# Linear attention with a decayed state: from tiles of 128 tokens to blocks of 64 on 64x64 tiles of TensorE

## The chip, the cores and the metric

The kernel runs on one core of one Trainium2 chip. The metric is the device time of one launch in microseconds (us). Before the change it was 674.69 and 676.3 us in two runs, median 675.5. The profile is one execution, recorded by the hardware's profiler, with a span of 672.5 us. TensorE's clock was granted in full throughout it (mean 0.999).

## The reference

Two operations follow each other. The first is attention with a decay per head: no softmax, but a 64x64 state per head which is faded and added to from block to block. The second is a mixer: a product of low rank along the tokens, and then two dense layers with a ReLU between them. B is 4, H is 8, S is 768 tokens, D is 64. Cut to what matters:

```python
def _attn_ref(q, k, v, lam):              # q, k, v: (4, 8, 768, 64), float32
    block = 64
    ...
    Dmask = np.where(rel >= 0, lam[:, None, None] ** rel[None, :, :], 0.0)
    lam_pow = lam[:, None, None] ** (pos[None, :, None] + 1)
    lam_block = lam ** block
    for b in range(nb):
        qb, kb, vb = (q[:, :, sl], k[:, :, sl], v[:, :, sl])
        intra = np.einsum('bhic,bhjc->bhij', qb, kb) * Dmask[None]
        intra = np.einsum('bhij,bhjd->bhid', intra, vb)
        inter = np.einsum('bhid,bhde->bhie', qb * lam_pow[None], kv_state)
        out[:, :, sl] = intra + inter
        rev_pow = lam[:, None, None] ** (block - 1 - pos[None, :, None])
        kb_dec = kb * rev_pow[None]
        kv_state = lam_block * kv_state + np.einsum('bhsd,bhse->bhde', kb_dec, vb)

def _moe_ref(x, U, V, w_ch1, w_ch2):      # x: (4, 768, 512), U: (768, 32), V: (32, 768)
    h = x.transpose(0, 2, 1) @ U @ V
    u = x + h.transpose(0, 2, 1)
    ch = np.maximum(u @ w_ch1, 0.0) @ w_ch2      # 512 -> 2048 -> 512
    return u + ch
```

The block length is free: the same output comes out of any split of the tokens, if the decay inside a block goes into the mask and the decay across blocks into the scaling of q and k and into the state.

## The kernel before

The attention is computed in 24 steps, one for each tile of 128 tokens (6 tiles in each of 4 batches, `NT = 6`, `NS = 24`). A tile holds all 8 heads, as 4 pairs (`HP = 4`). All on-chip sums of this part lie in one pool, in eight banks: one each for the tags `pq`, `pk`, `pt` and `pu`, two for the scores `pss`, two for the output `px`.

```python
def turn_half(s, a0, name):               # transposes of q or k, then a copy by ScalarE
    ts, tag = (qts, ("pq", "pt")) if name == "q" else (kts, ("pk", "pu"))
    ...
    nc.tensor.transpose(out=pt[:, a - a0, :], in_=raw[s, name][:, 2 * a : 2 * a + 2, :], identity=ident)
    nc.scalar.copy(ts[s][:, a0 : a0 + n, :], pt)

def scale_k(s):                           # GpSimd: k times its reversed decay; none for a batch's last tile
    ...
def scale(s):                             # GpSimd: q times its decay; none for a batch's first tile
    ...
def fade(s):                              # ScalarE: the state times lam**128, 4 operations
    if 0 < s % NT < NT - 1:
        ...
def scores(s):
    st[s]["pss"] = pss = two_banks("pss", "pss").rearrange("p x (a i) -> p x a i", a=HP)
    for a in range(HP):
        for x in range(2):
            for rows in half if s >= 2 * NT else [slice(0, P)]:
                nc.tensor.matmul(out=pss[rows, x, a, :], lhsT=kt[half[x], a, rows],
                                 rhs=qt[half[x], a, :], start=True, stop=True)
def masked(s):                            # VectorE, one operation for each of two banks
    for x in range(2):
        nc.vector.tensor_tensor(out=sm[:, x], in0=pss[:, x], in1=mask[:, x], op=ALU.mult)
def state(s):                             # none for a batch's last tile
    if c < NT - 1:
        pkv = one_bank([P, HP, D], "pkv", "pk")
        for a in range(HP):
            for x in range(2):
                nc.tensor.matmul(out=pkv[half[x], a, :], lhsT=ks[:, a, x, :], rhs=vr[:, 2 * a + x, :],
                                 start=True, stop=True)
        ...
            nc.vector.tensor_tensor(out=kv[s + 1], in0=pkv, in1=st[s]["faded"], op=ALU.add)
def inter(s):                             # state times q; none for a batch's first tile
    for a in range(HP):
        for x in range(2):
            for t in range(2):
                nc.tensor.matmul(out=px[half[t], x, a, :], lhsT=st[s]["qs"][half[x], a, half[t]],
                                 rhs=kv[s][half[x], a, :], start=(a == 0), stop=False)
def intra(s):                             # masked scores times v, on top of inter
    for a in range(HP):
        for x in range(2):
            for t in range(2):
                nc.tensor.matmul(out=px[half[t], x, a, :], lhsT=sm[:, x, a, half[t]],
                                 rhs=vr[:, 2 * a + x, :], start=(first and a == 0), stop=(a == HP - 1))
    nc.scalar.copy(xs[s].rearrange("p (a x e) -> p x a e", a=HP, x=2), px)
```

Seven steps behind the attention, each tile of x gets its low-rank part (`mix`: one matmul into the bank `pu` and an addition by VectorE) and is turned and split for the dense layers (`turn`: four transposes into the bank `pt`, then VectorE, ScalarE and GpSimd). At a batch's first tile, `low` forms the low-rank rows of the batch before in the bank `pq`; `low_rows` and three `next_of_low` split them into a high and a low part. The weights' conversion (`aside`) is spread over the steps. The order of emission is fixed, and is the order in which each engine works:

```python
    step = [("prep", s + 1), ("scale", s + 1)] * more
    step += [("mix", done)] * (0 <= done < NS - NT - 1)              # done = s - NT - 1
    step += [("low", b - 1), ("low_rows", b - 1)]                     # c == 0 and b > 0 alone
    step += [("intra", s), ("next_of_low", b - 1), ("late", s), ("state", s), ("next_of_low", b - 1)]
    step += [("turned", done - 1), ("late", s), ("next_of_low", b - 1), ("scores", s + 1)]
    step += [("aside", s)] * (s >= 2 * NT)
    step += [("inter", s + 1), ("masked", s + 1), ("fade", s + 1)]
    step += [("aside", s)] * (s < 2 * NT) + [("turn", done)]
```

(The conditions of most pieces are left out here.) After the 24 steps come the two dense layers: 48 units of the hidden layer with 24 matmuls each, and 384 rounds of three matmuls for the output layer, each matmul with 512 columns. The change doesn't touch them.

Of the kernel before, what the change touches and what calls it, by code (L numbers as in the profile page):

```python
# [8 lines left out]
FP32 = mybir.dt.float32  # L9
# [5 lines left out]
P = 128  # L15
# [3 lines left out]
def kernel(  # L19
# [227 lines left out]

    def one_bank(shape, name, tag):
        return psf.tile(shape, FP32, tag=tag, name=name)
# [14 lines left out]
    def load(name, s, engine):  # L264
        b, c = divmod(s, NT)
        t = raw_pool.tile(
            [P, H, D], FP32, tag=f"{name}raw", bufs=4 if name == "k" else 3, name=f"{name}raw"
# [19 lines left out]
    small = consts.tile([P, 16], FP32, name="small")  # L287
# [8 lines left out]
    lamc = powq[:, :, P - 1 : P]  # L296

    def constants():
        for a in range(HP):
            for x in range(2):  # L300
                h = 2 * a + x
                nc.vector.tensor_tensor_scan(
                    mask[:, x, a, :], lamb[:, h : h + 1].broadcast_to([P, P]), ident, 0.0,
                    ALU.mult, ALU.add,
                )

    def powers():
# [5 lines left out]
        for a in range(HP):  # L313
            nc.vector.tensor_tensor_scan(
                powq[:, a, :], lamh[:, a : a + 1].broadcast_to([P, P]),
                zeros.broadcast_to([P, P]), 1.0, ALU.mult, ALU.add,
            )

# [10 lines left out]
    kv = {}  # L329
# [10 lines left out]
    def turn_half(s, a0, name):  # L340

        ts, tag = (qts, ("pq", "pt")) if name == "q" else (kts, ("pk", "pu"))
        if a0 == 0:
            ts[s] = att.tile([P, HP, P], FP32, tag=name + "t", bufs=2, name=name + "t")
        n = HP // parts(s)
        pt = one_bank([P, n, P], "p" + name, tag[a0 > 0])
# [5 lines left out]

    def prep(s):
        for a0 in range(0, HP, HP // parts(s)):
            for name in "qk":
                turn_half(s, a0, name)
        st[s].update(qt=qts.pop(s), kt=kts.pop(s))
        for name in "qk":
            load_next(name)

    def scale_k(s):
        st[s] = {}
        if s % NT < NT - 1:
            st[s]["ks"] = ks = att.tile([P, HP, 2, D], FP32, tag="ks", bufs=2, name="ks")
# [7 lines left out]
    def scale(s):  # L372

        if s % NT > 0:
            st[s]["qs"] = qs = att.tile([P, HP, P], FP32, tag="qs", bufs=2, name="qs")
            nc.gpsimd.tensor_tensor(out=qs, in0=st[s]["qt"], in1=powq, op=ALU.mult)  # L376
        if s + 1 < NS:
            scale_k(s + 1)

    def fade(s):  # L380

        if 0 < s % NT < NT - 1:
            st[s]["faded"] = faded = att.tile([P, HP, D], FP32, tag="faded", name="faded")
            for a in range(HP):
                nc.scalar.mul(faded[:, a, :], kv[s][:, a, :], lamc[:, a, :])

    def scores(s):
        qt, kt = st[s]["qt"], st[s]["kt"]
        st[s]["pss"] = pss = two_banks("pss", "pss").rearrange("p x (a i) -> p x a i", a=HP)
        for a in range(HP):  # L390
            for x in range(2):
                for rows in half if s >= 2 * NT else [slice(0, P)]:
                    nc.tensor.matmul(  # L393
                        out=pss[rows, x, a, :], lhsT=kt[half[x], a, rows],
                        rhs=qt[half[x], a, :], start=True, stop=True,
                    )

    def masked(s):
        pss = st[s].pop("pss")
        st[s]["sm"] = sm = att.tile([P, 2, HP, P], FP32, tag="sm", bufs=1, name="sm")  # L400
        for x in range(2):
            nc.vector.tensor_tensor(out=sm[:, x], in0=pss[:, x], in1=mask[:, x], op=ALU.mult)  # L402

    def state(s):
        c = s % NT
        if c < NT - 1:
            ks, vr = st[s]["ks"], raw[s, "v"]
            pkv = one_bank([P, HP, D], "pkv", "pk")
            for a in range(HP):
                for x in range(2):  # L410
                    nc.tensor.matmul(  # L411
                        out=pkv[half[x], a, :], lhsT=ks[:, a, x, :], rhs=vr[:, 2 * a + x, :],
                        start=True, stop=True,
                    )
            kv[s + 1] = att.tile([P, HP, D], FP32, tag="kv", bufs=2, name="kv")
            if c == 0:
                nc.vector.tensor_copy(out=kv[s + 1], in_=pkv)
            else:
                nc.vector.tensor_tensor(out=kv[s + 1], in0=pkv, in1=st[s]["faded"], op=ALU.add)
        del st[s]  # L420
        del raw[s, "v"]
        load_next("v")

    def inter(s):

        st[s]["px"] = both = two_banks("px", "px")
        px = both[:, :, 0 : HP * D].rearrange("p x (a e) -> p x a e", a=HP)
        if s % NT == 0:
            return

        for a in range(HP):
            for x in range(2):
                for t in range(2):
                    nc.tensor.matmul(  # L434
                        out=px[half[t], x, a, :], lhsT=st[s]["qs"][half[x], a, half[t]],
                        rhs=kv[s][half[x], a, :], start=(a == 0), stop=False,
                    )

    def intra(s):
        first = s % NT == 0  # L440
        sm, vr, px = st[s]["sm"], raw[s, "v"], st[s]["px"]
        px = px[:, :, 0 : HP * D].rearrange("p x (a e) -> p x a e", a=HP)
        for a in range(HP):
# [514 lines left out]
```

## Time and profile before

| | us |
|---|---|
| device time, median of two runs | 675.5 |
| span of the profile | 672.5 |
| TensorE busy | 665.9 |
| VectorE busy | 496.6 |
| ScalarE busy | 278.7 |
| GpSimd busy | 112.8 |
| matmuls of scores (L393), both shapes | 28.1 |
| matmuls of masked scores times v (L446) | 28.3 |
| matmuls of the state (L411) | 12.9 |
| matmuls of state times q (L434) | 13.7 |
| masking of the scores (L402) | 30.8 |
| additions and copies to the state (L419, L417) | 8.5 |

Line numbers are those of the kernel before. A float32 matmul of this part is two instructions on TensorE: the 96 score matmuls of the first 12 tiles are 192 in the profile. In a row of the timeline or the groups, "128*64" names the rows and columns of the array that an instruction takes, and what follows is the data it reads; "x32" is the number of instructions. TensorE overlaps neighbouring instructions, so a group's duration there is longer than its distance to the next group's start, and the distances are what add up to a step. Busy times are sums over the whole span; a step's limit has to be read from the step.

### The profile page before, as it was taken

What the parts mean: (1) busy time and instruction counts of PE and PEld (TensorE: products, weight loads), DVE (VectorE), ACT (ScalarE), POOL (GpSimd) and SP (SyncE); (2) the same over time, 40 slices, a digit from 0 to 9 for tenths busy, and PEclk for the clock granted to TensorE, in tenths of its full rate; (3) what the DMA queues carried; (4) which work ended last, traced back from release to release, by engine and by line L of the source; (5) the groups of instructions that cost most, each with busy time, mean ns of one, the idle gap of its engine ahead of it and who ended that gap; (6) DMA issues with size and microseconds to landing.
All of it is one profiled execution on the core that took longest, in us unless ns stands there. A gap on an engine that the chain in (4) does not pass through costs nothing.

```text
span 672.5 us, 13170 instructions
## 1 busy us (share of the span) xinstructions
PE 665.9 (99%) x5124; PEld 545.4 (81%) x5124; DVE 496.6 (74%) x873; ACT 278.7 (41%) x517; POOL 112.8 (17%) x92
## 2 busy tenths in 40 slices
PE   9999999999999999999999999999999999999997
PEld 8888898787888888888888888888888888888885
DVE  4679999777999777777797255786586775865854
ACT  4675767454555444444455121332232322322320
POOL 4455667340000000000000000030030200300300
PEclk9999999999999999999999999999999999999999
DMA  9999993264776555555587999854363363443421
GB/s 208 214 228 239 237 232 109 84 215 156 235 276 240 204 203 204 204 203 204 203 280 253 325 314 387 291 185 140 94 206 107 110 204 94 158 155 95 161 89 62
DMA packets 131775, 131.27 MB, mean 195 GB/s; under 512 B 81346, under 2 KB 89794, under 8 KB 131714
## 3 DMA queue, kind: packets, MB, share of 16 engines
q1 hardware_dynamic: 130656, 130.18, 61.3%
q8 instruction: 40, 0.66, 0.4%
q10 hardware_dynamic: 1058, 0.26, 0.2%
q14 instruction: 21, 0.17, 0.1%
HBM read 80.09 MB, written 50.33 MB: 194 GB/s over the span
## 4 chain that ended last, share of the span: by engine, by line
PE 96%; DVE 2%; ACT 2%; issue 0%; DVEq 0%; ACTq 0%
PE pz L722 27%; PE pz L857 13%; PE pd L732 13%; PE pz L855 13%; PE pd L859 13%; PE pss L393 3%; PE px L446 3%; PE put L523 2%; PE pq L348 2%; PE px L434 1%; PE pkv L411 1%; PE pk L348 1%; PE pp L461 1%; PE pu L506 1%; PE idle L336 0%; ACT qt L351 0%
## 5 line engine op out<-in xcount | busy, mean ns | idle before, releaser
L722 PE MATMUL pz<-u_hl,w 128*128 128x512 f32 x768 | 190.4, 397 | 0.0
L722 PEld LDWEIGHTS pz<-u_hl,w 128*128 128x128 f32 x768 | 144.0, 188 | 35.5 <-issue 0.4
L857 PE MATMUL pz<-w_hl,m 128*128 128x512 f32 x384 | 151.1, 396 | 0.0
L855 PE MATMUL pz<-w_hl,m 128*128 128x512 f32 x384 | 150.9, 396 | 0.0
L859 PE MATMUL pd<-w_d,m 128*128 128x512 f32 x384 | 149.5, 396 | 0.0
L838 ACT ACTIVATE m<-mt 128x512 fp32r<-128x512 f32 x96 | 60.7, 633 | 196.0 <-PE pd L859 141.7
L839 DVE SCALAR_TENSOR_TENSOR m<-rm,m 128x512 fp32r<-128x512 f32 x96 | 71.4, 745 | 52.2 <-ACT m L838 52.1
L884 POOL TENSOR_TENSOR o<-o,u 128x512 f32<-128x512 f32 x20 | 29.9, 1529 | 447.3 <-DVE o L880 447.3
L737 DVE SCALAR_TENSOR_TENSOR r<-pd,r 128x512 f32<-128x512 f32 x96 | 61.8, 685 | 54.0 <-ACT r L728 43.5
L732 PE MATMUL pd<-u_d,w 128*128 128x512 f32 x384 | 98.6, 397 | 0.0
L728 ACT ACTIVATE r<-pz 128x512 f32<-128x512 f32 x96 | 52.2, 596 | 93.6 <-PE pz L722 92.9
L857 PEld LDWEIGHTS pz<-w_hl,m 128*128 128x128 f32 x384 | 72.3, 188 | 17.7
L855 PEld LDWEIGHTS pz<-w_hl,m 128*128 128x128 f32 x384 | 72.3, 188 | 17.6
L859 PEld LDWEIGHTS pd<-w_d,m 128*128 128x128 f32 x384 | 72.3, 188 | 17.6
L732 PEld LDWEIGHTS pd<-u_d,w 128*128 128x128 f32 x384 | 72.1, 188 | 17.3
L840 DVE SCALAR_TENSOR_TENSOR m<-m 128x512 fp32r<-128x512 f32 x96 | 69.0, 720 | 0.9
L837 DVE TENSOR_SCALAR mt<-rm 128x512 uint32<-128x512 uint32 x96 | 46.1, 481 | 28.0 <-DMA rm<-r_d 27.6
L402 DVE TENSOR_TENSOR sm<-pss,mask 128x512 f32<-128x512 f32 x48 | 30.8, 683 | 7.4 <-PE pss L393 7.3
L205 ACT CAST w<-wt 128x512 fp32r<-128x512 f32 x32 | 19.9, 622 | 30.5 <-DVE wt L202 23.4
L376 POOL TENSOR_TENSOR qs<-qt,powq 128x512 f32<-128x512 f32 x20 | 25.9, 1296 | 23.3 <-ACT qt L351 22.3
L446 PEld LDWEIGHTS px<-vraw,sm 128*64 128x64 f32 x768 | 24.7, 137 | 6.0 <-issue 2.4
L446 PE MATMUL px<-vraw,sm 128*64 128x64 f32 x768 | 28.3, 226 | 0.5 <-DVE sm L402 0.4
(88 smaller groups left out, 682.7 us busy)
## 6 DMA issues: line engine op xcount, KB each, us to landing
r_d<-r SPq DMA_DIRECT2D x96, 256.0 KB, 2.5
rm<-r_d SPq DMA_DIRECT2D x96, 256.0 KB, 2.7
words<-in_moe_w_ch_dram SPq DMA_DIRECT2D x30, 512.0 KB, 4.4
w_d<-w SPq DMA_DIRECT2D x16, 768.0 KB, 3.3
w_hl<-w_d SPq DMA_DIRECT2D x16, 512.0 KB, 6.2
vraw<-in_v_dram SPq DMA_DIRECT2D x24, 256.0 KB, 4.6
u_d<-x_nat SPq DMA_DIRECT2D x24, 256.0 KB, 3.5
u<-u_d SPq DMA_DIRECT2D x24, 256.0 KB, 4.1
```

Of the source, the lines that this page charges most:

```text
L446: nc.tensor.matmul(out=px[half[t], x, a, :], lhsT=sm[:, x, a, half[t]], rhs=vr[:, 2 * a + x, :], start=(first and a == 0), stop=(a == HP - 1),
L722: nc.tensor.matmul(out=acc[g][0], lhsT=w[:, n, ct, :], rhs=uhl[g][:, n, ct, :], start=(ct == 0 and n == 0), stop=(ct == CT - 1 and n == 1),)
L728: nc.scalar.mul(rs[g], acc[g][0], 4096.0 + 1.0)
L732: nc.tensor.matmul(out=acc[g][1], lhsT=w[:, 2, ct, :], rhs=ud[g][:, ct, :], start=(ct == 0), stop=(ct == CT - 1),)
L737: nc.vector.scalar_tensor_tensor(rs[g], acc[g][1], 4096.0, rs[g], ALU.mult, ALU.add)
L837: nc.vector.tensor_scalar(t.bitcast(U32), r.bitcast(U32), HI, None, ALU.bitwise_and)
L838: nc.scalar.activation(out=m[:, 0], in_=t, func=AF.Relu)
L839: nc.vector.scalar_tensor_tensor(m[:, 1], r, 0.0, hi, ALU.max, ALU.subtract)
L840: nc.vector.scalar_tensor_tensor(m[:, 2], hi, E, low, ALU.mult, ALU.subtract)
L855: nc.tensor.matmul(out=pz, lhsT=m[:, 0, cols], rhs=hl[:, 0], start=first, stop=False)
L857: nc.tensor.matmul(out=pz, lhsT=m[:, 1, cols], rhs=hl[:, 1], start=False, stop=end)
L859: nc.tensor.matmul(out=pd, lhsT=m[:, 2, cols], rhs=dd, start=first, stop=end)
```

## The change

The attention goes over to blocks of 64 tokens, two in a tile of 128. Scores and masked scores are then two 64x64 blocks on the diagonal of each head's 128x128, and the half that was masked away or lay across blocks is no longer computed. What crosses from the first block of a tile to the second goes through the state instead: a state `kvm` in the middle of the tile, beside the one at its end, `kv`. Both carry the decay to the end of the tile, and the second half of q's powers is divided by the decay of a block to match. So every tile has a state, the first of a batch has a state times q for its second half, and the last of a batch has a middle state.

All matmuls of the attention then take a quarter of the array, 64x64, and the aim is to have the four quarters work at a time. The banks are dealt out anew: the tags `pq` and `pk` become two halves of one tile `qk`, which holds q's transposes and k's, and then the scores in their place; the two halves of the state get banks of their own, `fz` and `fd`. Scaled q and k and their transposes have one buffer each instead of two; v has four instead of three. The state of the next tile and the scaling of its k move within the step, and the turn of a finished tile goes from the end of a step to the start of the next. Cut to its core:

```diff
+    qk = two_banks("qk", "qk")
     def one_bank(shape, name, tag):
-        return psf.tile(shape, FP32, tag=tag, name=name)
+        if tag not in ("pq", "pk"):
+            return psf.tile(shape, FP32, tag=tag, name=name)
+        ...
+        t = qk[:, tag == "pk", 0:n]
...
     def constants():
+        first = tmp("first")[:, 0:P]
+        nc.vector.memset(first[:, D:], 0.0)
+        nc.vector.tensor_tensor(out=first[:, 0:D], in0=ident[:, 0:D], in1=ident[:, D:], op=ALU.add)
...  (the 8 scans of the mask start from `first`; two copies make rev)
     def powers():
...  (scans over 64 columns)
+        nc.vector.reciprocal(out=lamc, in_=block)
+        nc.vector.tensor_tensor(out=powq[:, :, D:], in0=powq[:, :, 0:D], in1=lamc.broadcast_to([P, HP, D]), op=ALU.mult)
+        nc.vector.tensor_tensor(out=lamc, in0=block, in1=block, op=ALU.mult)
...
     def scores(s):
-                for rows in half if s >= 2 * NT else [slice(0, P)]:
+                for t in range(2):
                     nc.tensor.matmul(
-                        out=pss[rows, x, a, :], lhsT=kt[half[x], a, rows],
-                        rhs=qt[half[x], a, :], start=True, stop=True,
+                        out=pss[half[t], x, a, :], lhsT=kt[half[x], a, half[t]],
+                        rhs=qt[half[x], a, half[t]], start=True, stop=True,
     def masked(s):
-        for x in range(2):
-            nc.vector.tensor_tensor(out=sm[:, x], in0=pss[:, x], in1=mask[:, x], op=ALU.mult)
+        nc.vector.tensor_tensor(out=sm, in0=pss, in1=mask[:, :, :, 0:D], op=ALU.mult)
     def state(s):
+        ts = range(2 if c < NT - 1 else 1)
+        pkv = [one_bank([P, HP, D], "pkv", ("fz", "fd")[t]) for t in ts]
...
+                for t in ts:
+                    nc.tensor.matmul(out=pkv[t][half[x], a, :], lhsT=ks[half[t], a, x, :],
+                                     rhs=vr[half[t], 2 * a + x, :], start=True, stop=True)
...
+            nc.vector.tensor_tensor(out=kvm, in0=pkv[0], in1=faded.pop(s), op=ALU.add)
+        if c < NT - 1:
+            nc.vector.tensor_tensor(out=kv[s + 1], in0=pkv[1], in1=kvm, op=ALU.add)
     def inter(s):
+                for t in range(s % NT == 0, 2):
+                    held = st[s]["kvm"] if t else kv[s]
...
     def intra(s):
-        for a in range(HP):
-            for x in range(2):
+        for x in range(2):
+            for a in range(HP):
                 for t in range(2):
                     nc.tensor.matmul(
-                        out=px[half[t], x, a, :], lhsT=sm[:, x, a, half[t]],
-                        rhs=vr[:, 2 * a + x, :], start=(first and a == 0), stop=(a == HP - 1),
+                        out=px[half[t], x, a, :], lhsT=sm[half[t], x, a, :],
+                        rhs=vr[half[t], 2 * a + x, :], start=(first and t == 0 and a == 0), stop=(a == HP - 1),
...
+        step = [("scale_k", s + 1)] + [("turn", done - 1)] + [("prep", s + 1, "q")]
+        step += [("mix", done)] + [("prep", s + 1, "k"), ("scale", s + 1)]
+        step += [("low", b - 1), ("low_rows", b - 1)]
+        step += [("intra", s), ("next_of_low", b - 1), ("late", s), ("state", s + 1), ("next_of_low", b - 1)]
+        step += [("turned", done - 1), ("late", s), ("next_of_low", b - 1)]
+        both = [("scores", s + 1), ("inter", s + 1)]
+        step += both[::-1] if s + 2 == NS else both
+        step += [("masked", s + 1), ("fade", s + 2), ("aside", s)]
```

(In the last block the conditions are left out, as above.)

## The prediction

> **What bounds the kernel now.** I began with the page's busy shares and its chain of waits.
>
> ```profile
> PE 665.9 (99%) x5124; PEld 545.4 (81%) x5124; DVE 496.6 (74%) x873; ACT 278.7 (41%) x517; POOL 112.8 (17%) x92
> PE 96%; DVE 2%; ACT 2%; issue 0%; DVEq 0%; ACTq 0%
> ```
>
> TensorE is busy 99% of the span and carries 96% of the chain, so whatever leaves TensorE shortens the kernel, provided that no other engine is just behind it. The change touches only the attention front, the first 121 us (the timeline has the last masked-scores product at 120.29 us); the 550 us of products after it keep their instructions. So the question is settled in 24 steps, one for each tile of 128 tokens. The view by windows shows two steps of the first batch (18 to 27 us) and two of the last (107 to 116 us):
>
> ```profile
> core 0: us, PE busy (x) PEld busy (x) DVE busy (x) ACT busy (x) POOL busy (x), PEclk, DMA share, GB/s
> 18.35:27.30 8.95, 8.90 (x211) 7.91 (x212) 4.74 (x12) 6.17 (x17) 3.61 (x3) 1.00 0.88 205
> 107.00:116.50 9.50, 9.50 (x253) 8.75 (x254) 9.14 (x16) 6.84 (x19) 6.82 (x5) 1.00 0.29 88
> ```
>
> Early, only TensorE is full. Late, VectorE is at 9.14 of 9.50: a second bound, 4% behind. Next the timeline of one late step, 86.70 to 91.44 us (columns: start, duration, engine and line):
>
> ```profile
> 86.70 1.15 PE L446 MATMUL px<-vraw,sm 128*64 128x64 f32 x32
> 87.69 0.64 PE L411 MATMUL pkv<-vraw,ks 128*64 128x64 f32 x16
> 88.25 1.10 PE L393 MATMUL pss<-qt,kt 64*64 64x128 f32 x32
> 88.44 0.42 DVE L419 TENSOR_TENSOR kv<-pkv,faded 128x256 f32<-128x256 f32 x1 [0.52 <-PE pkv L411]
> 89.18 0.64 PE L434 MATMUL px<-kv,qs 64*64 64x64 f32 x32
> 89.64 1.27 DVE L402 TENSOR_TENSOR sm<-pss,mask 128x512 f32<-128x512 f32 x2
> 89.75 0.66 PE L523 MATMUL put<-ident,x_nat 128*128 128x128 f32 x4
> 90.25 0.60 PE L348 MATMUL pq<-ident,qraw 128*128 128x128 f32 x4
> 90.68 0.60 PE L348 MATMUL pk<-ident,kraw 128*128 128x128 f32 x4
> 91.04 0.47 PE L506 MATMUL pu<-vp 128*128 128x512 f32 x1
> 91.44 1.15 PE L446 MATMUL px<-vraw,sm 128*64 128x64 f32 x32
> ```
>
> From start to start: masked scores times v 0.99, state 0.56, scores 0.93, state times q 0.57, turn of x 0.50, turn of q 0.43, turn of k 0.36, mix 0.40; together 4.74 us, without a gap. Masking (89.64 to 90.91) lies beside the turns, because the scores have banks of their own. In the first batch, without turn of x and mix, a step takes 4.28 us (products by v start at 23.01 and 27.30 on the chain).
>
> **What the Trainium skill says.** "TensorEngine Tiling (Array Packing)", section Key Properties, has it that different tiles run matmuls in parallel. The rows above agree: 32 instructions on four 64x64 tiles, 64 columns each, take 0.57 us, 18 ns each; 32 on two 128x64 tiles take 0.99, 31 ns each. The same page, section PSUM Bottleneck, warns that tiling speeds up TensorE but not the emptying of PSUM; one state addition on VectorE took 0.42 us here, nearly as long as its matmuls. "PSUM — Partial Sum Buffer", section PSUM bank collisions, says that a bank being read may not be written by another engine meanwhile. So turns that share a bank with scores must wait for the mask. No wait of this kind is in the trace of before, where the scores have their own banks.
>
> **The change, part by part.** TensorE first, in a late step. Scores: 32 instructions of 64x128 become 32 of 64x64 on four tiles, the shape of state times q: 0.93 to 0.57, so 0.36 saved. Products by v: the same 32 instructions, but each reads 64 rows and its row half is also its column half, so just two tiles take turns, as two do now; I leave it at 0.99. State: 16 become 32 over four tiles, 0.56 to 0.57. Sum 4.39 instead of 4.74.
>
> VectorE: masking is one operation of 0.68 instead of two (1.27), but the state needs two additions, 0.42 each, instead of one. So a regular step changes by -0.59 + 0.42 = -0.17, which would bring 9.14 per two steps to about 8.8.
>
> Now the waits. Emission puts both additions ahead of the mask on VectorE, and the next turn of q overwrites the bank that the mask reads. From the start of the state's matmuls: they issue for 0.57, the last ends 0.08 later (as 0.64 against 0.56 shows), VectorE starts 0.11 later (88.33 to 88.44): 0.76. Two additions: 1.60. Mask: 2.28. About 0.10 to TensorE: 2.38. There the turn of q starts, then 0.43 + 0.40 + 0.36 + 0.99 to the next state: 4.56 us. This ring is longer than TensorE's 4.39, and it takes the step: 0.18 saved rather than 0.35. In the first batch, without turn of x and mix, TensorE needs 3.49 but the ring 4.16, against 4.28: 0.12 saved.
>
> Whole front:
> - Regular steps: about 16 at 0.15, 2.4 us. The second batch goes at 4.95 now (46.68 to 51.64 to 56.59 on the chain) because its scores still use 64x128 tiles; another 0.5. One wait of 0.37 for the scaled q at 21 us should go. Sum -3.3.
> - First tile of a batch: it had no state times q, so its step was 4.17; the ring makes it 4.56: three times +0.4. Last tile of a batch: it had no state update and now has one of 16 instructions and one addition: four times +0.2. Sum +2.0.
> - Start: the mask needs a sum ahead of its scans, powers need a reciprocal and a product, the first tile now needs a state and an inter product before its successor's turns. Some 0.5 us more on VectorE by its rows (copies of 0.14, an addition of 0.42) and about 0.9 on TensorE less what the scores save: +1.0.
> - Low-rank rows: at a batch's first tile their product lands in the bank of q's turn, which is now the scores' bank too. They are split off by four operations (1.22 us at 67.54) and four more (1.25 at 69.25). Today nothing on TensorE waits for the second four but the next turn of q. After, the second four come after the state's additions (1.60 + 1.25 = 2.85), the scores wait for them, end at about 3.6, the mask at 4.3, and the turn of q starts at 4.4 instead of 2.4: +2.0, twice (batches two and three). The first batch's go by a copy: +0.5. Sum +4.5.
>
> Total -3.3 + 2.0 + 1.0 + 4.5 = +4.2, so 679.7; I say 679.5.
>
> **Rivals.** (a) TensorE's saving comes through whole and the products by v run at the pace of four tiles, because two diagonal tiles share neither rows nor columns. That is 0.42 more for each of 24 steps, on the ring itself: -10 us, of which VectorE lets pass about eight, as its own 4.4 per late step is near. Result about 670. For it: different row halves. Against: the early scores alternate two row halves as well and took 1.09 for 16 instructions of twice the columns, 68 ns, no better per column than the 31 to 34 of the 128x64 tiles. (b) The ring is longer than I think: VectorE arrives late, still at the weights' conversion (one such operation, L179, took 1.28 at 60.57 on the chain, against 0.70 in its group's mean), so that the mask and with it the turn of q slips. GpSimd gets two more operations per batch (1.06 and about 0.7) and single buffers for its scaled q and k. At 0.3 per step over 20 steps, 686. (c) Loading bounds the front: the share of the DMA engines is 0.88 to 1.02 in these windows. In the list of waits nothing in the front idles longer than 0.9 us in all for a load of q, k or v, and steps barely shorten here, so this would cost at most what the steps save. (d) No rows-to-scores wait as reckoned, if VectorE reaches them early: -4, about 675.5.
>
> **Range and chances.** The steps' sum has an uncertain term of up to -8 (a), one of -4 (d), and +6 (b); run to run the time before went over 1.6 us. From these: 8 in 10 between 670 and 687, a little more room above. Two per cent are 13.5 us: under 662 all of (a) and more would have to hold, 0.03; above 689 (b) would have to be twice as bad, 0.09; within, 0.88.
>
> **What would show it.** Right: scores rows of 64 columns at 0.57 to 0.62 per step; TensorE idle ahead of the turn of q, put down to the mask; two of the steps at batch starts with TensorE idle ahead of the scores, put down to the row operations on VectorE; late steps near 4.56; the first product of the hidden layer about 4 us later than 121.45. Wrong: products by v under 0.8 us per step (then (a)), or late steps above 4.8 (then (b)), or DMA named ahead of turns (c). After the front, the products should take the same 551 us.

## The result and the profile after

The changed kernel takes 703.55 us (702.83 and 704.26 in two runs) against 675.5: a ratio of 1.0417, 95% interval 1.0378 to 1.0456. It is slower by 28 us. 679.5 was predicted, and at most 687 in the range: the prediction was wrong. The page of the changed kernel, busy shares and chain:

```profile
PE 669.3 (95%) x5764; PEld 541.8 (77%) x5764; DVE 496.4 (71%) x879; ACT 285.7 (41%) x533; POOL 121.0 (17%) x100
PE 92%; DVE 3%; ACT 3%; issue 1%; DVEq 0%; ACTq 0%
```

The span went from 672.5 to 701.0 us, 28.5 more, but TensorE is busy only 3.4 us longer. So TensorE waits where it didn't before. All of it lies in the attention front: the first product of the hidden layer starts at 150.18 us in the timeline, against 121.45 before, and from there to the end it takes 550.8 us, as before.

The list of waits of the changed kernel says for what (columns: engine, tile and line that waited, what it waited for; us in total, times, longest):

```profile
PE qk L375 <- ACT qt L378: 13.4, 24, 0.7
PE qk L415 <- DVE vp L512: 4.6, 2, 2.3
PE qk L375 <- DVE sm L423: 3.5, 6, 1.4
PE qk L486 <- ACT kt L378: 2.2, 3, 0.7
PE px L456 <- DVE kvm L439: 2.0, 4, 1.5
```

The first row is half of the loss, and nothing in the prediction speaks of it. L375 is a turn, L378 ScalarE's copy of its result, and there are 24 tiles: in every step a turn waits for the copy of *q*. Those five rows sum to 25.7 us. Added up over the timeline, all idle time of TensorE in the front (gaps over 0.05 us, without 1.1 us at the very start that both kernels have) is 26.7 us, against 1.6 before; with the 3.4 us of busy time that gives 28.5.

The timeline of one late step shows which turn (start, duration, engine and line; what ended the idle time stands in brackets):

```profile
95.81 0.65 PE L375 MATMUL qk<-ident,qraw 128*128 128x128 f32 x4
...
96.55 0.59 ACT L378 COPY qt<-qk 128x512 f32<-128x512 f32 x1 [0.23 <-issue]
97.19 0.66 PE L375 MATMUL qk<-ident,kraw 128*128 128x128 f32 x4 [0.49 <-ACT qt L378]
97.78 1.08 PE L467 MATMUL px<-vraw,sm 64*64 64x64 f32 x29
...
98.65 0.27 PE L433 MATMUL pkv<-vraw,ks 64*64 64x64 f32 x1
...
99.22 0.63 PE L415 MATMUL qk<-qt,kt 64*64 64x64 f32 x30
99.52 0.42 DVE L441 TENSOR_TENSOR kvm<-pkv,faded 128x256 f32<-128x256 f32 x1 [0.93 <-PE pkv L433]
99.70 0.29 PE L456 MATMUL px<-kv,qs 64*64 64x64 f32 x2
100.00 0.27 PE L456 MATMUL px<-kvm,qs 64*64 64x64 f32 x1
...
100.05 0.42 DVE L444 TENSOR_TENSOR kv<-pkv,kvm 128x256 f32<-128x256 f32 x1
100.39 0.68 DVE L423 TENSOR_TENSOR sm<-qk,mask 128x512 f32<-128x512 f32 x1
100.57 1.06 ACT L407 ACTIVATE faded<-kv,small 128x64 f32<-128x64 f32 x4 [0.49 <-DVE kv L444]
100.62 0.65 PE L548 MATMUL put<-ident,x_nat 128*128 128x128 f32 x4
101.13 0.66 PE L375 MATMUL qk<-ident,qraw 128*128 128x128 f32 x4
```

q's turn is issued at 95.81, its copy ends at 97.14, and k's turn starts at 97.19. Yet k's turn writes another bank than the one that ScalarE reads. Both banks belong to one tile, `qk`, so the reading is that the wait is for the tile; the experiments test it. From start to start the step is 5.32 us, where 4.56 was predicted: from the state to the next turn of q 2.48 (predicted 2.38), from q's turn to the products by v 1.97 (predicted 0.43 + 0.40 + 0.36 = 1.19), and the products by v 0.87 (predicted 0.99).

Where the 28.8 us of the front come from, by the distances between the starts of the products by v (first at 9.62 us before and 13.42 after, last at 120.29 and 149.10):

| | before | after | difference | predicted |
|---|---|---|---|---|
| up to the first product, and the first step | 13.99 | 19.75 | +5.8 | +1.0 |
| 15 regular steps | 72.28 | 79.97 | +7.7 | -3.3 |
| the six steps around three batch starts | 30.15 | 45.14 | +15.0 | +6.5 |
| last step | 3.87 | 4.24 | +0.4 | |

6.5 is the sum of +2.0 for first and last tiles and +4.5 for low-rank rows.

### The profile page after: what moved, and what is told of

The parts are those of the page before. It is cut to its first block, busy times and chain, and to the rows that moved or that the text cites. A ratio compares the mean times of both kernels' runs of the same rounds, so it can differ in the third digit from the quotient of the medians.

```text
span 701.0 us, 14563 instructions
## 1 busy us (share of the span) xinstructions
PE 669.3 (95%) x5764; PEld 541.8 (77%) x5764; DVE 496.4 (71%) x879; ACT 285.7 (41%) x533; POOL 121.0 (17%) x100
## 4 chain that ended last, share of the span: by engine, by line
PE 92%; DVE 3%; ACT 3%; issue 1%; DVEq 0%; ACTq 0%
PE pz L750 26%; PE pz L883 13%; PE pz L885 13%; PE pd L760 13%; PE pd L887 13%; PE px L467 4%; PE qk L375 3%; ACT qt L378 2%; PE px L456 2%; PE put L548 2%; PE pkv L433 1%; PE qk L415 1%; DVE sm L423 1%; PE qk L486 1%; DVE kvm L441 0%
## 5 line engine op out<-in xcount | busy, mean ns | idle before, releaser
L387 POOL TENSOR_TENSOR ks<-kraw,small 128x512 f32<-128x512 f32 x24 | 30.1, 1253 | 18.0 <-issue 10.3
L398 POOL TENSOR_TENSOR qs<-qt,powq 128x512 f32<-128x512 f32 (+1 forms) x24 | 28.7, 1194 | 20.1 <-ACT qt L378 18.2
L441 DVE TENSOR_TENSOR kvm<-pkv,faded 128x256 f32<-128x256 f32 x20 | 8.5, 425 | 30.8 <-PE pkv L433 30.4
L375 PE MATMUL qk<-ident,kraw 128*128 128x128 f32 x94 | 16.2, 296 | 13.4 <-ACT qt L378 13.4
```

## The experiments

The theory after this reading, A: the loss comes from making one tile of the banks for q's turn and k's turn. k's turn then waits for the copy of q, and q's turn for the mask of all scores; two waits in one ring. Rivals: B, that the loss comes from the blocks of 64 (more instructions, two additions, a middle state); C, that single buffers of scaled and turned q and k hold the step. Each ratio below is to the kernel before, and the code shows the lines that matter, with ... for the rest.

### The kernel before with one shared tile

```diff
+    qk = two_banks("qk", "qk")             # tags pq and pk are its halves, as in the changed kernel
-        st[s]["pss"] = pss = two_banks("pss", "pss").rearrange("p x (a i) -> p x a i", a=HP)
+        st[s]["pss"] = pss = qk.rearrange("p x (a i) -> p x a i", a=HP)
-            pkv = one_bank([P, HP, D], "pkv", "pk")
+            pkv = one_bank([P, HP, D], "pkv", "fz")
```

> The kernel before (tiles of 128 tokens) with one part of the change alone: scores in the one tile that also holds the turns of q and k, and the state's sums in a bank of their own. Theory A (sharing one tile makes the turn of k wait for the copy of q, and the turn of q for the mask): a late step goes from 4.74 to about 5.9 us (1.97 from the turn of q to the products by v, 0.99, 0.56, 1.01, mask 1.42), an early one from 4.28 to about the same; about 30 us more, near 705. Theory B (the cost lies in the blocks of 64: more operations on VectorE and GpSimd, two tiles in turn): this kernel has none of them, so it stays under 684.

Measured: 728.07 us, ratio 1.0800 (1.0779 to 1.0822). Tiles of 128 tokens with the sharing lose more than blocks of 64 with it, so the sharing alone is enough for a loss of this size. That the blocks of 64 cost nothing besides is not shown by it. The list of waits of this kernel (L356 the turns, L359 their copies, L410 the mask):

```profile
PE qk L356 <- ACT qt L359: 17.0, 24, 0.7
PE qk L356 <- DVE sm L410: 16.5, 23, 1.5
PE qk L401 <- DVE vp L495: 3.6, 2, 1.8
```

The copy of q holds a turn 24 times here too, and the mask holds q's turn 23 times, as expected. The loss was larger than the 30 us expected. Late steps take 6.33 to 6.83 us in place of 5.9: in one of 6.83 VectorE is still at a weights' operation (158.78 to 160.08 us) when the scores are done at 159.35, so the mask starts at 160.00. And TensorE's clock was granted at 0.50 in 13.7 us of the front, which costs at most 6.8 us.

### The same with two tiles

```diff
-    qk = two_banks("qk", "qk")
+    qk = [psf.tile([P, N], FP32, tag=t, name=t) for t in ("pq", "pk")]
```

Nothing else is changed but the indexing that follows from it: the same banks, the same order, the same scores in the turns' banks.

> The run before_shared (the kernel before, its scores in the banks of the turns) with the two banks as two tiles. There TensorE idled 16.9 us ahead of the turns of k for the copy of q and 16.5 us ahead of the turns of q for the mask. Theory A: the first kind goes, and half of the mask's wait, as the turn of q now waits for the first of two mask operations alone; the turn of k may wait for the second. About 25 us less than 728, so 700 to 706. Rival (the banks are what is short, however they are named): 720 or more.

Measured: 684.81 us, ratio 1.0159 (1.0139 to 1.0179), 43 us less. The list of waits:

```profile
PE pq L356 <- DVE sm L410: 5.2, 12, 0.8
PE pq L401 <- DVE vp L495: 3.8, 2, 1.9
```

The row with the copy of q is gone, and of the waits for the mask 5.2 us are left, since q's turn now waits only for the first of two masks. This pair is the clearest evidence for the mechanism of A: one declaration, and 43 us. The waits for the copy and the mask fall by 28.3 us, near the 25 expected for the whole. TensorE's busy time falls by 13.4 us more (682.2 to 668.8). About half of that is the half clock, which this profile does not have in the front; the other half is not explained.

### The changed kernel with two tiles

```diff
-    qk = two_banks("qk", "qk")
+    qk = [psf.tile([P, N], FP32, tag=t, name=t) for t in ("pq", "pk")]
...
-        nc.vector.tensor_tensor(out=sm, in0=pss, in1=mask[:, :, :, 0:D], op=ALU.mult)
+        for x in range(2):
...
+            nc.vector.tensor_tensor(out=sm[:, x], in0=pss, in1=mask[:, x, :, 0:D], op=ALU.mult)   # pss: bank x
```

A one-element matmul, `tie`, which reads the turned q, is added ahead of the products by v. State times q and masked scores times v write the same banks from different quarters of the array; the wait for q's copy had kept them in order, and `tie` is there to keep it. So the products by v still wait for the copy of q in this kernel and in every later one with `tie`.

> The changed kernel with the banks of q's and k's turns as two tiles instead of one, so that the turn of k no longer waits for the copy of q (the masking becomes two operations of half the size; a matmul of one element that reads the turned q keeps the order of two writers of the output's bank). Theory A: the turn of k starts 0.4 us (without mix) or 0.8 (with it) after that of q instead of 1.38; a late step goes from 5.32 to about 4.6, the whole to about 685. Theory B: 700 or more, as blocks and operations are the same. Theory C (the half clock of TensorE after its waits at the start and at 46 us is most of it): about 695.

Measured: 695.59 us, ratio 1.0319 (1.0298 to 1.0339): 8 us of the 28 (6.6 by the two ratios). The list of waits (L468 is `tie`):

```profile
PE pq L415 <- DVE vp L520: 4.6, 2, 2.3
PE px L457 <- DVE kvm L440: 3.0, 3, 2.3
PE tie L468 <- ACT qt L378: 2.7, 7, 0.6
```

The 13.4 us are gone, and clean late steps (no other wait at a batch start, full clock) take 4.78 us in place of 5.32. But less came of it than expected. What remains are the waits at batch starts and at the start, 3.6 us of idle time that the profile puts down to no releaser ("issue"), and three stretches at half the clock (10.5 to 13.9, 82.2 to 89.0 and 119.7 to 123.1 us). The measured time is what the expectation gave for its third theory, half clock as most of the loss. The profile speaks against "most": 13.7 us at 0.50 cost at most 6.8 us, of 21.4 by which this front is longer than that of the kernel before.

### The mask ahead of the second addition

```diff
-        if c < NT - 1:
-            nc.vector.tensor_tensor(out=kv[s + 1], in0=pkv[1], in1=kvm, op=ALU.add)
+    def end_state(s):                      # the same addition, emitted behind ("masked", s + 1)
```

> The changed kernel with one thing moved: VectorE masks the scores before it adds the second half of the state, not after. If the ring state - addition - addition - mask - turn of q sets the step (theory A, second part), each step loses one addition of 0.42 us less what TensorE needs for scores and state times q anyway: about 0.3 over 23 steps, so about 696. If the step is set by something else, the time stays at 703.

Measured: 707.34 us, ratio 1.0493 (1.0462 to 1.0523). A miss: the mask is earlier, but regular steps go from 5.31 to 5.52 us, and the waits for the copy of q grow from 13.4 to 19.4 us. Something else had come into the ring; `both_rings` below shows what.

### The turn of x between the turns of q and k

```diff
-        step += [("turn", done - 1)] * turns
         step += [("prep", s + 1, "q")] * more
+        step += [("turn", done - 1)] * turns
```

> The changed kernel with the turn of a finished x moved from ahead of the turn of q to between the turns of q and k, where TensorE stands idle 0.48 us for the copy of q. Theory A (a ring sets the step: mask - turn of q - copy of q - turn of k - products by v - state - additions - mask; the mask ends at 2.42 us after the state's start, just when TensorE reaches the turn of q): the idle time moves to ahead of the turn of q, now put down to the mask, and a late step stays at 5.3 us; 702 to 704. Rival (the idle time ahead of the turn of k is a hole that other work can fill): 0.48 saved in 15 steps, about 696.

Measured: 703.81 us, ratio 1.0441 (1.0405 to 1.0477); a late step stays at 5.32 us. TensorE is given work for the time in which k's turn waits, and the idle time moves to q's turn. The list of waits:

```profile
PE qk L375 <- DVE sm L423: 8.4, 18, 1.4
PE qk L375 <- ACT qt L378: 6.6, 10, 0.7
```

So it is a ring that sets the step (a chain of operations through several engines that leads from each step to the next), not a hole in TensorE's order. In the changed kernel early steps, without a turn of x, and late ones have the same 5.31 us for that reason.

### Two buffers for turned and scaled q and k

```diff
-            ts[s] = att.tile([P, HP, P], FP32, tag=name + "t", name=name + "t")
+            ts[s] = att.tile([P, HP, P], FP32, tag=name + "t", bufs=2, name=name + "t")
```

The same for `ks` and `qs`.

> The changed kernel with two buffers again for the turned q and k and the scaled q and k, as the kernel before has. Theory A: none of the waits that TensorE spends is for a buffer of these, so the time stays at 702 to 704. Rival (single buffers hold up GpSimd's scaling and ScalarE's copies, and through them TensorE): 690 to 697.

Measured: 704.27 us, ratio 1.0448 (1.0421 to 1.0474), late steps of 5.32 us as before. C is refuted.

### Both rings at once

The mask ahead of the second addition and the turn of x between the turns, together.

> The changed kernel with both rings cut at once: the mask ahead of the second state addition on VectorE, and the turn of x between the turns of q and k. Theory (one shared tile makes two rings, state to mask to turn of q, and turn of q to copy to turn of k; each cut alone only moved the idle time to the other): together they should shorten late steps, which have a turn of x, from 5.32 to about 4.9, some 14 of them: about 698 us, with the idle time ahead of q's turn under 3 us and ahead of k's turn under 9. Rival (the first cut gained nothing because the late second addition makes the state's fade on ScalarE late, which then delays the copies of q and k): the step stays at 5.2 or above and the time at 702 to 707, with the copies of q as what TensorE waits for.

Measured: 709.66 us, ratio 1.0506 (1.0462 to 1.0549), late steps of 5.52 us. The rival named there holds. The timeline of a late step:

```profile
96.67 0.69 DVE L423 TENSOR_TENSOR sm<-qk,mask 128x512 f32<-128x512 f32 x1 [0.82 <-PE qk L415]
...
97.28 0.42 DVE L447 TENSOR_TENSOR kv<-pkv,kvm 128x256 f32<-128x256 f32 x1
97.42 0.66 PE L375 MATMUL qk<-ident,qraw 128*128 128x128 f32 x4 [0.35 <-DVE sm L423]
...
97.79 1.07 ACT L407 ACTIVATE faded<-kv,small 128x64 f32<-128x64 f32 x4 [1.12 <-DVE kv L447]
...
98.76 0.56 ACT L378 COPY qt<-qk 128x512 f32<-128x512 f32 x1
...
99.38 0.65 PE L375 MATMUL qk<-ident,kraw 128*128 128x128 f32 x4 [0.64 <-ACT qt L378]
```

q's turn is done by 98.08, but ScalarE is still fading the state: that began late, because its input, the second addition, was put behind the mask. The copy of q waits for the fade, and k's turn for the copy. This also explains the miss with the mask alone.

### The third ring: the fade behind the copies

```diff
-        step += [("masked", s + 1), ("end_state", s + 1), ("fade", s + 2)] * more
+        step += [("masked", s + 1), ("end_state", s + 1)] * more
-        step += [("prep", s + 1, "k"), ("scale", s + 1)] * more
+        step += [("prep", s + 1, "k")] * more + [("fade", s + 1)] * (more and s > 0) + [("scale", s + 1)] * more
```

On top of the two cuts before.

> The changed kernel still with one tile for both turns, the mask ahead of the second state addition, the turn of x between the turns of q and k, and the state's fade on ScalarE moved from ahead of the copy of q to behind the copy of k. Theory (there are three rings over the shared tile; with the first two cut, the fade of 1.07 us, which waits for the later second addition, stood ahead of the copy of q and held k's turn): in late steps the wait ahead of k's turn vanishes and a late step takes 4.5 to 4.8 us in place of 5.52; the early steps, without a turn of x, keep a wait of about 0.7 us ahead of k's turn. With about 13 late steps: 696 to 700 us in place of 709.7. Rival (the copies are late for another reason, such as ScalarE's other work or the port to PSUM): the wait stays above 0.5 us in late steps and the time above 703.

Measured: 699.52 us, ratio 1.0360 (1.0328 to 1.0391), clearly below `both_rings`; against the changed kernel the two intervals just overlap. Clean late steps take 4.91 us, where the changed kernel's take 5.32. The timeline of one:

```profile
98.75 0.69 DVE L423 TENSOR_TENSOR sm<-qk,mask 128x512 f32<-128x512 f32 x1
...
99.54 0.66 PE L375 MATMUL qk<-ident,qraw 128*128 128x128 f32 x4
...
100.27 0.59 ACT L378 COPY qt<-qk 128x512 f32<-128x512 f32 x1 [0.98 <-PE qk L375]
100.39 0.47 PE L536 MATMUL pu<-vp 128*128 128x512 f32 x1
100.91 0.66 PE L375 MATMUL qk<-ident,kraw 128*128 128x128 f32 x4
```

With the fade out of the way the copy starts as soon as q's turn has ended (100.20), and ends at 100.86, as does the mix: TensorE no longer idles ahead of k's turn. The waits for q's copy fall to 6.0 us, nine times, in early steps, as expected. The step is 0.11 above the range expected, because the ring is shorter and not gone: the mask ends at 99.44, q's turn starts 0.10 later, and from there the copy leads to k's turn as before.

### The rows ahead of the additions

```diff
-        step += [("late", s)] * (s < NT - 1 or s == NT) + [("state", s + 1)] * more
         step += [("next_of_low", b - 1)] * (c == 0 and b > 0)
+        step += [("late", s)] * (s < NT - 1 or s == NT) + [("state", s + 1)] * more
```

> The changed kernel with the second four row operations on VectorE (the low part of the low-rank rows) ahead of the state's two additions in place of behind them, at the first tile of batches two to four. Theory (scores wait for these four operations because they land in the bank of the scores, and the operations queue behind the additions): the two waits of 2.28 us ahead of the scores shrink to about 1.4 each, the additions come later by as much, so what the order alone is worth is 1 to 2 us: about 702. If the half clock that follows such waits hangs on their length, it may go too: then 699 to 700. Rival (the row operations are held by something else, the product itself): the waits stay at 2.3 and the time at 703.5.

Measured: 700.80 us, ratio 1.0393 (1.0362 to 1.0424). The ratio's interval overlaps that of the changed kernel; the list of waits decides:

```profile
PE qk L415 <- DVE vp L512: 2.3, 2, 1.2
```

Two waits of 2.28 us are now two of 1.16. This profile has no half clock in the front. With two tiles as well:

> The changed kernel with two tiles for q's and k's turns, plus the row operations ahead of the state's additions. With two tiles alone it took 695.6 us and the two waits of 2.28 us ahead of the scores were followed by half a clock for some 10 us in all. Theory: each wait shrinks to about 1.4, and if the half clock comes from idle time, it shortens too: 691 to 693. Rival (the half clock is not tied to these waits): 694 to 695, with as much half clock as before.

Measured: 692.17 us, ratio 1.0257 (1.0232 to 1.0282). The waits for the rows fall to 1.5 us in both together, and the granted clock of this profile is 1.00 throughout the front, so the rival with as much half clock as before did not hold in it. What it has instead is idle time without a releaser, 5.8 us in all, such as the 2.12 us ahead of a turn of x:

```profile
94.96 0.49 PE L556 MATMUL put<-ident,x_nat 128*128 128x128 f32 x3 [2.12 <-issue]
```

### Are blocks of 64 faster once nothing is shared?

Three versions try it. `own_scores` gives the scores banks of their own again and puts the state's sums into the banks of the turns; the rows' product goes to `pt`, q's turn ahead of the turn of x, and `tie` is kept:

```diff
-        pss = qk[:, :, 0 : HP * D].rearrange("p x (a i) -> p x a i", a=HP)
+        st[s]["pss"] = pss = two_banks("pss", "pss")[:, :, 0 : HP * D].rearrange("p x (a i) -> p x a i", a=HP)
...
-        pkv = [one_bank([P, HP, D], "pkv", ("fz", "fd")[t]) for t in ts]
+        pkv = [one_bank([P, HP, D], "pkv", ("pq", "pk")[t]) for t in ts]
```

> Blocks of 64 as in the changed kernel, but banks as in the kernel before: scores in two banks of their own, the two halves of the state in the banks of q's and k's turns, the low-rank rows in the bank of x's turn, and the turn of q ahead of that of x. Theory A: no turn waits for the mask or for a copy of the other bank any more; a late step is near TensorE's sum or VectorE's, 4.4 to 4.6 us; the whole lies at 675 to 680, level with the kernel before. Theory B: blocks of 64 are slow by themselves, 690 or more.

Measured: 692.68 us, ratio 1.0271 (1.0250 to 1.0292). A had been given 675 to 680, B 690 or more: by its own measure this run speaks for B. With nothing shared, 19 us of loss remain. In `own_scores2` the rows' product moves behind the products by v, into the bank `pu`, and the copies that reverse k's decay behind the powers:

> The run own_scores with three of its remaining waits attacked: the low-rank rows come after the products by v and lie in the bank of the mix (there TensorE waited 2.55 us for VectorE in two steps), and GpSimd's first scaling comes after VectorE's powers (beside it two copies of 64x4 took 1.21 us instead of 0.32). Clean late steps stay at 4.66. Expected 692.7 - 2.5 - 1.5 (half clock after a wait of 1.9 us) - 1 = about 688. If blocks of 64 can win at all, it would have to come under 674 here.

Measured: 690.85 us, ratio 1.0241 (1.0221 to 1.0262), 3 us above what was expected and 17 above the kernel before. Clean late steps take 4.66 us, against 4.74 before: the gain per step is 0.08. The last, `two_tiles_fade`, is the version with two tiles and early rows, with the fade behind the copies:

> The changed kernel with two tiles for the turns, the row operations ahead of the state's additions (692.2 us so far), and the fade behind the copy of k as well. Theory (blocks of 64 tokens gain next to nothing per step and pay at the start and at batch starts, whatever the order): the 3.0 us for which the products by v wait for the copy of q go down to about 1, so 689 to 691, still slower than before. Rival (the whole loss was in waits that sharing made, and the blocks as such are faster): 670 to 680.

Measured: 693.03 us, ratio 1.0254 (1.0219 to 1.0290): no different from two tiles with early rows. TensorE's waits for the copy of q are down to 1.4 us and the clean late step is still 4.78 us. No version of blocks of 64 came below the kernel before; nor did sharing with tiles of 128.

The same distances as in the table above, for one profile of each kernel, show where the loss goes and where it stays (the kernel before in us, the others as differences to it):

| | up to the first product, and the first step | 15 regular steps | six steps around batch starts |
|---|---|---|---|
| before | 13.99 | 72.28 | 30.15 |
| changed kernel | +5.8 | +7.7 | +15.0 |
| `two_tiles` | +4.2 | +3.8 | +13.1 |
| `two_tiles_rows` | +4.9 | +7.1 | +5.9 |
| `own_scores2` | +4.3 | +1.1 | +11.3 |

So A holds for the regular steps: with banks of their own they lose 1.1 us in place of 7.7. At the start and the batch starts most of the loss stays without any sharing, and comes with the blocks of 64 and their order: this is B's part, and the larger one, 17.1 of 28.8 us, though 4.0 us of waits ahead of `tie` are in it. `two_tiles_rows` brings the batch starts below the +6.5 that was predicted; of the 7.2 us there against `two_tiles`, up to 4.8 are half clock that only the profile of `two_tiles` has. Its regular steps are held by 5.9 us of idle time without a releaser and 2.1 us ahead of `tie`. The banks of `own_scores2` with the order of `two_tiles_rows` were not tried. The longest waits of TensorE in `own_scores2` (L455 is `tie`):

```profile
PE tie L455 <- ACT qt L364: 4.0, 9, 0.8
PE px L444 <- DVE kvm L429: 3.3, 5, 1.4
PE pss L403 <- issue: 2.5, 4, 0.8
PE pu L526 <- ACT vp L516: 2.0, 3, 0.7
```

The idle time without a releaser can be placed. The page lists a queue of instruction transfers, first for the kernel before, then for `own_scores2`:

```profile
q8 instruction: 40, 0.66, 0.4%
q8 instruction: 46, 0.75, 0.5%
```

These are transfers of 16 KB, 40 and 46 of them. The traces have 10366 and 11752 instructions of TensorE (PE and PEld, those of the sequencer included), which are 40.5 and 45.9 times 256. So the queue brings TensorE its own instructions, about 256 at a time. In the fronts of all the profiles here, from 12 us on, there are 44 waits over 0.15 us without a releaser. Counted along TensorE's instructions, 41 of them stand a multiple of 256 apart, to within one instruction, and 40 of the 41 end 1.26 to 1.64 us after a transfer has ended. So TensorE has most likely run out of instructions there; no run was made to test it. The kernel before has none of these waits, the changed kernel 0.3 us, the versions with two tiles or banks of their own 3.1 to 6.2 us. They issue more instructions than the kernel before, and wait less for other things than the changed kernel.

## Why the prediction was wrong, point by point

**The bound and where to look: right.** The change acts in the front alone, and the products after it take the same time.

**Shapes on TensorE: right but for one.** Scores take 0.54 us to the next group (predicted 0.57), the state 0.51 (0.57), products by v 0.87 (0.99). Rival (a), 0.57 for the products by v, fell: two diagonal quarters run at 0.87 / 32 = 27 ns for each instruction, between the 31 of two 128x64 tiles and the 18 of four quarters. State times q takes 0.92 in place of 0.57: its second half needs `kvm`, which VectorE adds from 99.52 to 99.94, and the matmuls go on at 100.00. That wait is a direct result of putting the middle state in, and the sum of 4.39 had no term for it. Without it and the wait of 0.49 for q's copy, the step's matmuls would sum to 5.32 - 0.49 - 0.35 = 4.48.

**VectorE: right.** Additions of 0.42 and one mask of 0.68, 4.25 us busy in this step of 5.32.

**The ring: its first part right, its second part the step that failed.** State to turn of q was reckoned at 2.38 and is 2.48. Then the prediction says: "There the turn of q starts, then 0.43 + 0.40 + 0.36 + 0.99 to the next state". That takes the turn of k to follow TensorE's order freely, as in the kernel before. But q's turn, its copy and k's turn are three links of the ring: 0.74 from the start of q's turn to the start of the copy, 0.59 for the copy, 0.05 to k's turn, together 1.38 where 0.43 (early) or 0.83 (late, with the mix) was set. From k's turn to the products by v it is 0.59 rather than 0.36. The 0.36 was k's turn to the mix; in early steps of the kernel before, where the products by v follow k's turn directly, it is 0.53 too:

```profile
9.09 0.60 PE L348 MATMUL pk<-ident,kraw 128*128 128x128 f32 x4
9.62 1.24 PE L446 MATMUL px<-vraw,sm 128*64 128x64 f32 x32
```

The ring is then 2.48 + 1.38 + 0.59 + 0.87 = 5.32, early and late. "PSUM — Partial Sum Buffer", PSUM bank collisions, was used to find a wait where a bank is shared; it speaks of banks, and the waits here go by the tile that was declared: the pair with 43 us between them shows it. The diff had it in plain sight: the line that makes one tile `qk` of two banks.

Of the 24 us by which the prediction missed, 11.0 lie in the regular steps, 8.5 at the batch starts and 4.8 at the start.

**Regular steps, -3.3: wrong in sign, +7.7.** All through the ring: TensorE idles 10.2 us in them, against 0.9 before, and without shared banks they lose 1.1. That the turn of q would be held by the mask was right for early steps (0.44 us each); late, TensorE comes to it at the same time (mask ends 101.07, turn 101.13).

**Batch starts, +6.5: +15.0.** The two waits for rows are 2.28 us each, where 2.0 were set: this part of the working holds. Not seen were the rows' product waiting for the copy of k, again because of the one tile (0.73, three times), the ring's waits in these six steps, and 1.35 us ahead of the turn of q at the first of the three, where the mask stood behind the rows' operations on VectorE (the mask starts at 53.06, right after the second of them). All idle time in these steps sums to 12.2 us. Only in part is this the sharing: `own_scores2` still loses 11.3 us here.

**The start, +1.0: +5.8.** TensorE is idle 3.9 us in it: 1.53 for `kvm` and the rest for the ring. `kvm` is late since VectorE's chain to the powers is: two copies of 64x4 numbers take 1.21 us (6.33 to 7.54) beside an operation of GpSimd (6.28 to 7.34), where two such copies took 0.32 before, not beside one. Those copies alone do not set the start, though: in `own_scores2` they took 0.33 and the first product with `kvm` still started at 10.62 us, against 10.37, for GpSimd's operation then came later. The rest is half a clock. The windows of the changed kernel:

```profile
core 0: us, PE busy (x) PEld busy (x) DVE busy (x) ACT busy (x) POOL busy (x), PEclk, DMA share, GB/s
12.00:16.00 4.00, 3.62 (x78) 3.30 (x82) 0.00 (x0) 1.47 (x3) 1.27 (x1) 0.57 1.00 191
46.00:50.00 4.00, 3.31 (x60) 2.76 (x62) 0.00 (x0) 1.08 (x4) 0.59 (x1) 0.57 0.64 137
```

The granted clock is 0.57 in these 8 us; before, it was 1.00 in the same windows. By estimate, what TensorE was busy with for 6.93 us would take 6.93 x 0.57 = 4.0 us at the full clock, so about 3 us are lost, 1.6 of them at the start.

**Rivals (b), (c), (d):** none held. The sign set for (b), late steps above 4.8, came true at 5.32, but not for its reason: VectorE is late with the mask at one batch start only. No turn waits for a load. The rows hold the scores, against (d). The range was too narrow because every rival was a size on the road that had been drawn; none asked whether a wait had been missed.

**What stays open.** What each of the waits at the start and the batch starts is worth without the sharing: in `own_scores2` those for `kvm`, for the rows' second half and for the copy of q are seen, but no run removes them one by one. And how much the blocks of 64 could gain at best: 0.08 us in a clean late step was reached, with `tie` in it.

## What to carry to other kernels

When two buffers become two halves of one tile, go through every reader and writer of either half: a wait that was between two operations on one bank comes to lie between all operations on both. Reckon a step as a ring through all engines (turn, copy, turn, product, state, mask) and not only as the sum on the busiest one; filling one hole in TensorE's order moved the idle time and left the step at 5.32 us. Cutting a ring by moving an operation back can put what depends on it into another one, as the fade did. And smaller tiles of TensorE mean more instructions: once the other waits are gone, the transfers of TensorE's own instructions can be the next.

## What the runs showed of the hardware

In the front of these kernels TensorE's clock was granted at 0.50 in stretches of 3.4 or 6.8 us: two in the changed kernel (from 12.3 and 46.4 us), none in the kernel before, in `before_two_tiles`, in `rows_early` and in `two_tiles_rows`. The rows' product of 48 matmuls took 2.79 us at 46.69 us in place of 1.52. "TensorE: Matmul & The Clock Gate", section Part 1: The HAM clock gate, says that a gate passes 4 of 8 pulses depending on how busy the array has lately been; the trace agrees in the factor. No rule for this case comes out of the traces: in `two_tiles` half a clock began within the first idle stretch of 2.28 us and 1 us after the second, in the changed kernel two such stretches had none, and its half clock at 46.4 us began in a wait of 0.74 us. It also differs between executions of one kernel: the means over the span were 0.995 and 0.998 in the two of the changed kernel.

"SBUF — State Buffer", section SBUF: two separate sides, says that VectorE and GpSimd share a pair of ports which, for certain operations of VectorE, one of them holds for a whole instruction while the other waits. The traces agree. In the changed kernel a copy of 64x4 numbers started at 6.33 us, during an operation of GpSimd from 6.28 to 7.34, and took 1.03 us, up to 7.36; the next took 0.17. In `own_scores` the first copy started before GpSimd's operation and took 0.16, the second started during it and took 0.97. In `two_tiles_rows` and `own_scores2` GpSimd's operation came later, and both copies took 0.16 to 0.17.
